# Grouped-query softmax attention: a first Q load in three pieces, fewer warm-up matmuls, and a last normalisation and store on other engines

## The chip, the cores and the metric

The kernel runs on one core of one Trainium2 chip. The metric is the device time of one execution in microseconds (us), median of several runs.

## The reference, cut to what matters

```python
B, Hq, Hkv, Sq, Sk, D = 16, 16, 8, 384, 384, 256       # all bf16
def reference(q, k, v):
    k = jnp.repeat(k, 2, axis=1); v = jnp.repeat(v, 2, axis=1)
    scores = jnp.einsum("bhqd,bhkd->bhqk", q, k) * D ** -0.5
    p = softmax(scores, axis=-1)
    return jnp.einsum("bhqk,bhkd->bhqd", p, v)
```

There are 128 **head pairs** (a batch and a kv head, with its two query heads). Each has six **units** of 128 query rows, 768 units in all. The pipeline works in **steps** of two units, 384 steps, three to a head pair. In the prediction "p=1" is the second head pair; "the last pair" and "the first tail pair" there mean two units, a step.

## The kernel before

Each engine has its own program, and semaphores tie them together. For one step: PE multiplies Q by K (scores S), DVE takes the negative row maximum (`negm`), ACT takes the exponential, PE transposes the result, DVE copies it out of PSUM, PE multiplies it by V (O, with a column of ones in V giving the row sum), ACT evicts O to SBUF, DVE takes the reciprocal of the row sum, POOL multiplies, and POOL stores to DRAM once per head pair. SP issues all loads. POOL also multiplies K by the scale.

```python
QB = KB = VB = 3; ...; NWARM = 24; KS_LEAD = 4         # cut
# SP: per head pair p
sp.dma_start_transpose(KTsb[:, p % KB], k[b, kvh]).then_inc(sem_k[p % KB], 16)
sp.dma_start_transpose(QTsb[:, p % QB], q[...]).then_inc(sem_q[p % QB], 16)
sp.dma_start(Vsb[:, p % VB, :, 0:D], v[...]).then_inc(sem_v[p % VB], 16)
# PE
for _w in range(NWARM):
    pe.matmul(psum[:, 7, 0:512], lhsT=ones[:, 0:128], rhs=ones[:, 0:512], ...)
for i in range(0, ND + 3):                             # do_S(i), do_O(i-2), do_PT(i-1); cut
# DVE, step i:  copy of P (i-2), reciprocal (i-3), max (i)
# ACT, step i:  two exponentials (i-1), then the eviction of O (i-2):
act.activation(out=Of32[:, ..., 0:D + 1], in_=psum[:, b0:b0 + 2, OOFF:OOFF + D + 1], func=ACT.Identity)
# POOL
pool.tensor_scalar(out=Osb[...], in0=Of32[...], scalar1=recip[:, g:g + 1], ...)     # norm of unit g
if g % UPP == UPP - 1:                                 # last unit of the head pair
    pool.wait_ge(sem_norm, g + 1)
    pool.dma_start(out[b, ...], Osb[:, p % OB]...).then_inc(sem_ost[p % OB], 16)
...
for s in range(OB):                                    # POOL's last act: all stores landed
    pool.wait_ge(sem_ost[s], 16 * n)
```

## Time and profile before

| | before |
|---|---|
| time, median of the first 4 runs | 651.22 us |
| span of the profiled run | 649.4 us |
| PE busy | 639.9 us (99%) |
| start of the first scores | 8.54 us |
| start of the second head pair's scores (step 3) | 13.32 us |
| start of the last step's scores | 638.42 us |
| from there to the end | 10.98 us |

From the page of the kernel before, the busy time of each engine, with its share of the span and its number of instructions:

```profile
PE 639.9 (99%) x6168; PEld 513.1 (79%) x6168; DVE 599.1 (92%) x1536; ACT 592.8 (91%) x1153; POOL 557.9 (86%) x1031
```

PE bounds the middle. A step takes 1.645 us there (median distance between the scores of neighbouring steps), and from the second head pair's scores to the last step's scores it is 638.42 - 13.32 = 625.10 us. Nothing in the change touches that stretch. What can move is the 13.3 us in front and the 11.0 us behind.

The start, from the timeline of the kernel before. The columns are start (us), length (us), engine (SPq is SP's sequencer, where the length is the time that issuing took), line, operation, tiles, shape and count; neighbours of one kind are merged:

```profile
0.80 1.32 SPq L98 DMA_TRANSPOSE KTsb<-in_k_dram  x1
1.38 7.33 PE L163 MATMUL psum<-ones 128*128 128x512 bf16 x24 [1.38 <-POOL ones L111]
2.18 1.46 SPq L99 DMA_TRANSPOSE QTsb<-in_q_dram  x1
...
5.59 1.92 SPq L99 DMA_TRANSPOSE QTsb<-in_q_dram  x1
...
8.54 1.46 PE L175 MATMUL psum<-KTsb,QTsb 128*128 128x384 bf16 x8
...
13.32 0.81 PE L175 MATMUL psum<-KTsb,QTsb 128*128 128x384 bf16 x4
```

The first Q was issued at 2.18 us and landed 4.04 us later, at 6.22. The scores began only at 8.54, right behind the last warm-up matmul. So the warm-ups held the start back, not the data. The second Q, issued at 5.59, landed at 9.91, over three microseconds before its use at 13.32.

The end, from the timeline of the kernel before:

```profile
638.42 0.81 PE L175 MATMUL psum<-KTsb,QTsb 128*128 128x384 bf16 x4
...
640.42 1.04 ACT L266 ACTIVATE Psb<-psum,negm 128x384 bf16<-128x384 f32 x2
...
642.00 0.83 PE L204 MATMUL psum<-Vsb,PTsb 128*128 128x257 bf16 x6
...
643.77 0.93 POOL L133 TENSOR_SCALAR Osb<-Of,recip 128x256 bf16<-128x256 f32 x2 [0.29 <-DVE recip L243]
644.99 0.76 POOL L140 DMA_DIRECT2D out_dram<-Osb  x1 [0.30 <-POOL Osb L133]
```

And from its view of DMA issues, the last store alone (KB, then us from issue to landing):

```profile
out_dram<-Osb POOLq DMA_DIRECT2D x1, 384.0 KB, 2.9
```

The store landed at 647.88 us. A **drain** (DRAIN) is a sequencer instruction that each engine has once at the kernel's end, recorded at line 49. The view of that line shows POOL's, with its length in ns and its start in us:

```profile
L49 POOLq DRAIN  x1: 1056/1056/1056, 648.1 to 648.1; - x1
```

### The profile page before, as it was taken

The page shows a single profiled execution, that of the slowest core. Times are in us where ns is not written, and L with a number is a line of the kernel's source. Part 1 is how long each engine was busy: PE and PEld are TensorE (multiplying, and loading weights), DVE is VectorE, ACT ScalarE, POOL GpSimd, SP SyncE. Part 2 cuts the span into 40 slices and gives each one's busy share as a digit, 9 for nine tenths or more (in the row PEclk, how much of TensorE's full clock was granted, in tenths as well). Part 3 has the DMA queues.
Part 4 walks back from the last instruction along what each step waited for, and adds up shares of the span by engine and source line. Part 5 has one row for each costly group of instructions (what it writes and reads, how often), then busy time and mean ns, then how long its engine had stood idle before and what let it go on. Part 6 is the DMA issues. An engine that isn't in the chain of part 4 may idle for free. (4 is left out here: it accounts for less than half of the span.)

```text
span 649.4 us, 18750 instructions
## 1 busy us (share of the span) xinstructions
PE 639.9 (99%) x6168; PEld 513.1 (79%) x6168; DVE 599.1 (92%) x1536; ACT 592.8 (91%) x1153; POOL 557.9 (86%) x1031
## 2 busy tenths in 40 slices
PE   8999999999999999999999999999999999999995
PEld 4888888888888888888888888888888888888884
DVE  3999999999999999999999999999999999999995
ACT  3999999999999999999999999999999999999995
POOL 3878898898888888889888988988888898898886
PEclk9999999999999999999999999999999999999999
DMA  8999999999999999999999999999999999999992
GB/s 164 207 222 268 233 235 261 240 226 266 231 226 262 223 254 224 265 233 223 245 254 234 229 266 238 223 266 230 237 255 232 240 228 267 234 225 259 236 218 97
DMA packets 368735, 152.23 MB, mean 234 GB/s; under 512 B 307200, under 2 KB 358400, under 8 KB 368640
## 3 DMA queue, kind: packets, MB, share of 16 engines
q1 hardware_dynamic: 354304, 100.70, 87.0%
q0 software_dynamic: 14336, 50.34, 21.2%
q8 instruction: 50, 0.82, 0.6%
q14 instruction: 45, 0.37, 0.2%
HBM read 25.17 MB, written 50.33 MB: 116 GB/s over the span
## 5 line engine op out<-in xcount | busy, mean ns | idle before, releaser
L266 ACT ACTIVATE Psb<-psum,negm 128x384 bf16<-128x384 f32 x768 | 401.0, 578 | 8.3 <-DVE negm L251 8.3
L251 DVE TENSOR_REDUCE negm<-psum 128x2 f32<-128x768 f32 x384 | 367.6, 958 | 42.3 <-PE psum L175 9.7
L133 POOL TENSOR_SCALAR Osb<-Of,recip 128x256 bf16<-128x256 f32 x768 | 353.0, 473 | 20.2 <-DVE recip L243 2.6
L204 PE MATMUL psum<-Vsb,PTsb 128*128 128x257 bf16 x2304 | 316.1, 273 | 0.5 <-DVE PTsb L235 0.3
L175 PE MATMUL psum<-KTsb,QTsb 128*128 128x384 bf16 x1536 | 312.2, 326 | 0.0
L204 PEld LDWEIGHTS psum<-Vsb,PTsb 128*128 128x128 bf16 x2304 | 225.2, 98 | 66.9 <-DVE PTsb L235 0.8
L277 ACT ACTIVATE Of<-psum 128x514 f32<-128x514 f32 x384 | 231.0, 602 | 41.6 <-PE psum L204 1.7
L235 DVE COPY PTsb<-psum 128x384 bf16<-128x384 bf16 x768 | 235.2, 348 | 1.1 <-PE psum L190 0.9
L190 PE MATMUL psum<-ident,Psb 128*128 128x128 bf16 x2304 | 191.6, 219 | 1.1 <-ACT Psb L266 1.0
L175 PEld LDWEIGHTS psum<-KTsb,QTsb 128*128 128x128 bf16 x1536 | 140.4, 103 | 45.9
L190 PEld LDWEIGHTS psum<-ident,Psb 128*128 128x128 bf16 x2304 | 160.8, 97 | 11.2 <-ACT Psb L266 1.7
L140 POOL DMA_DIRECT2D out_dram<-Osb x128 | 97.5, 762 | 41.0 <-POOL Osb L133 37.4
L122 POOL TENSOR_SCALAR KTsb<-KTsb 128x768 bf16<-128x768 bf16 x128 | 106.3, 830 | 26.0 <-DMA KTsb<-in_k_dram 16.2
L243 DVE RECIPROCAL recip<-Of 128x2 f32<-128x2 f32 x384 | 59.8, 156 | 1.2 <-ACT Of L277 1.2
L163 PE MATMUL psum<-ones 128*128 128x512 bf16 x24 | 7.3, 478 | 1.4 <-POOL ones L111 1.4
L163 PEld LDWEIGHTS psum<-ones 128*128 128x128 bf16 x24 | 2.8, 119 | 5.4 <-issue 2.7
L266 ACT ACT_TABLE_LOAD x1 | 1.3, 1283 | 0.8 <-PEq L294 0.8
L111 POOL MEMSET ones<- 128x512 bf16 x1 | 0.5, 524 | 0.3 <-POOLq L294 0.3
L294 POOL MEMSET const-float32-0.0<- 128x1 f32 x1 | 0.1, 93 | 0.3 <-issue 0.3
L114 POOL TENSOR_SCALAR_AFFINE_SELECT ident<-ones 128x128 bf16<-128x128 bf16 x1 | 0.3, 291 | 0.1
L112 POOL MEMSET Vsb<- 128x72 bf16 x1 | 0.2, 161 | 0.0
L294 POOL MEMSET const-uint8-127<- 128x1 uint8 x1 | 0.1, 96 | 0.0
(2 smaller groups left out, 0.2 us busy)
## 6 DMA issues: line engine op xcount, KB each, us to landing
out_dram<-Osb POOLq DMA_DIRECT2D x128, 384.0 KB, 4.2
Vsb<-in_v_dram SPq DMA_DIRECT2D x128, 192.0 KB, 3.8
KTsb<-in_k_dram SPq DMA_TRANSPOSE x128, 4.2
QTsb<-in_q_dram SPq DMA_TRANSPOSE x128, 4.8
```

The costliest lines, as they stand in the source:

```text
L122: pool.tensor_scalar(out=kt_ap, in0=kt_ap, scalar1=scale, scalar2=1.0, op0=ALU.mult, op1=ALU.mult,).then_inc(sem_ks, 1)
L133: pool.tensor_scalar(out=Osb[:, p % OB, j, t, :], in0=Of32[:, g % OFB, 0:D], scalar1=recip[:, g:g + 1], scalar2=1.0, op0=ALU.mult, op1=ALU ...
L140: pool.dma_start(out[b, kvh * REP:(kvh + 1) * REP].rearrange("h (p t) d -> p h (t d)", p=128), Osb[:, p % OB].rearrange("p h t d -> p h (t ...
L163: pe.matmul(psum[:, 7, 0:512], lhsT=ones[:, 0:128], rhs=ones[:, 0:512], start=True, stop=True)
L175: ins = pe.matmul(psum[:, sbank, 0:Sk], lhsT=QTsb[:, p % QB, dt, j * Sq + t: (j + 1) * Sq: QT], rhs=KTsb[:, p % KB, dt, :], start=(dt == 0 ...
L190: ins = pe.transpose(psum_bf[:, bank, kt * 128:(kt + 1) * 128], Psb[:, g % PB, kt * 128:(kt + 1) * 128], ident[:],)
L204: ins = pe.matmul(psum[:, bank, OOFF:OOFF + D + 1], lhsT=PTsb[:, g % PTB, kt, :], rhs=Vsb[:, p % VB, kt, 0:D + 1], start=(kt == 0), stop=( ...
L235: dve.tensor_copy(out=PTsb[:, g % PTB].rearrange("p a b -> p (a b)"), in_=psum_bf[:, PTO_BANK0 + g % NPTO, 0:KT * 128],).then_inc(sem_ptev, 1)
L243: dve.reciprocal(out=recip[:, g:g + 2], in_=Of32[:, g % OFB:g % OFB + 2, D:D + 1],).then_inc(sem_recip, 1)
L251: dve.tensor_reduce(out=negm[:, g:g + 2], in_=psum[:, b0:b0 + 2, 0:Sk], axis=AX.X, op=ALU.max, negate=True,).then_inc(sem_max, 1)
L266: act.activation(out=Psb[:, g % PB, :], in_=psum[:, S_BANK0 + g % NSB, 0:Sk], func=ACT.Exp, bias=negm[:, g:g + 1], scale=1.0,).then_inc(se ...
L277: act.activation(out=Of32[:, g % OFB:g % OFB + 2, 0:D + 1], in_=psum[:, b0:b0 + 2, OOFF:OOFF + D + 1], func=ACT.Identity,).then_inc(sem_oc, 1)
```

## The change

Its intent is to shorten both ends. In front: 14 warm-ups instead of 24; the first head pair's Q in three loads (128, 256 and 384 rows), so that its first unit could start early; and no wait for POOL's scaling of the first K, the scale being applied on ACT instead, to `negm` and in the exponential. Behind: the last three steps are normalised on ACT directly from PSUM, with DVE's reciprocal also from PSUM, and the last head pair is stored by SP, one store per head. The diff, cut to its core:

```diff
-    NWARM = 24
+    NWARM = 14
+        Q0_PIECES = [(0, 0, 128), (0, 128, Sq)] + [(j, 0, Sq) for j in range(1, REP)]
+        TAIL0 = NU - UPP
 # SP
+                if p == 0:
+                    for i, (j, r0, r1) in enumerate(Q0_PIECES):
+                        sp.dma_start_transpose(
+                            QTsb[:, 0, :, j * Sq + r0:j * Sq + r1], q[b, kvh * REP + j, r0:r1, :]
+                        ).then_inc(sem_q0[i], 16)
 ...
+            for j in range(REP):                       # the last head pair, one store per head
+                sp.wait_ge(sem_tn, QT * (j + 1))
+                sp.dma_start(out[b, kvh * REP + j]..., Osb[:, pl % OB, j]...).then_inc(sem_ostt[j], 16)
+            for j in range(REP):
+                sp.wait_ge(sem_ostt[j], 16)
 # POOL
+                if g >= TAIL0:
+                    return                             # no norm and no store of the last head pair
-                if e % DPP == 0 and e // DPP < NP:
+                if e % DPP == 0 and 1 <= e // DPP < NP:    # the first K is not scaled
                     do_ks(e // DPP)
-                n = len([p for p in range(NP) if p % OB == s])
+                n = len([p for p in range(NP - 1) if p % OB == s])
 # DVE, step i, after the max
+                if 0 <= e < ND and 2 * e >= TAIL0:     # e = i - 2
+                    for g in (2 * e, 2 * e + 1):
+                        dve.reciprocal(out=recip[:, g:g + 1], in_=psum[..., OOFF + D:OOFF + D + 1])
 # ACT, the first three steps
+                                act.activation(out=negm0[:, g:g + 2], in_=negm[:, g:g + 2], func=ACT.Identity, scale=scale)
+                                act.activation(out=Psb[...], in_=psum[...], func=ACT.Exp, bias=negm0[:, g:g + 1], scale=scale)
 # ACT, the last three steps, after the exponentials
+                        act.activation(out=Osb[:, p % OB, j, t, :], in_=psum[..., OOFF:OOFF + D],
+                                       func=ACT.Identity, scale=recip[:, g:g + 1])
```

Left out: the first head pair's row order and the store that fits it, and the waits of PE that follow from all this.

More of the change, by code (lines that the diff above doesn't have):

```diff
@@ L88, in bass_standalone__gqa_softmax__near_ridge_kernel, with q0_piece, q_count @@
         sem_norm = sem("sem_norm")
+        Q0_PIECES = [(0, 0, 128), (0, 128, Sq)] + [(j, 0, Sq) for j in range(1, REP)]
+        sem_q0 = [sem(f"sem_q0_{i}") for i in range(len(Q0_PIECES))]
+        sem_at = sem("sem_at")
+        negm0 = sb("negm0", [128, UPP], F32)
+        def q0_piece(j, t):
+            for i, (jj, r0, r1) in enumerate(Q0_PIECES):
+                if jj == j and r0 <= t * 128 < r1:
+                    return i
+            raise AssertionError
+        sem_rct = sem("sem_rct")
+        sem_tn = sem("sem_tn")
+        sem_ostt = [sem(f"sem_ostt{j}") for j in range(REP)]
+        TAIL0 = NU - UPP
+        def q_count(p):
+            n = p // QB + 1
+            if p % QB == 0:
+                n -= 1
+            return 16 * n
         block = es.enter_context(nc.Block())
@@ L98, in _ @@
                 sp.dma_start_transpose(KTsb[:, p % KB], k[b, kvh]).then_inc(sem_k[p % KB], 16)
-                sp.dma_start_transpose(
-                    QTsb[:, p % QB], q[b, kvh * REP:(kvh + 1) * REP].rearrange("h s d -> (h s) d")
-                ).then_inc(sem_q[p % QB], 16)
+                if p == 0:
[3 more added lines that the diff above has]
+                        ).then_inc(sem_q0[i], 16)
+                else:
+                    sp.dma_start_transpose(
+                        QTsb[:, p % QB], q[b, kvh * REP:(kvh + 1) * REP].rearrange("h s d -> (h s) d")
+                    ).then_inc(sem_q[p % QB], 16)
                 if p >= VB:
@@ L107, in _ @@
                 ).then_inc(sem_v[p % VB], 16)
+            pl = NP - 1
+            b, kvh = pair_bh(pl)
+            for j in range(REP):
+                sp.wait_ge(sem_tn, QT * (j + 1))
+                if pl == 0:
+                    sp.dma_start(
+                        out[b, kvh * REP + j].rearrange("(t p) d -> p t d", p=128),
+                        Osb[:, pl % OB, j],
+                    ).then_inc(sem_ostt[j], 16)
+                else:
+                    sp.dma_start(
+                        out[b, kvh * REP + j].rearrange("(p t) d -> p (t d)", p=128),
+                        Osb[:, pl % OB, j].rearrange("p t d -> p (t d)"),
+                    ).then_inc(sem_ostt[j], 16)
+            for j in range(REP):
+                sp.wait_ge(sem_ostt[j], 16)
         @block.gpsimd
@@ L139, in do_norm @@
                     pool.wait_ge(sem_norm, g + 1)
-                    pool.dma_start(
-                        out[b, kvh * REP:(kvh + 1) * REP].rearrange("h (p t) d -> p h (t d)", p=128),
-                        Osb[:, p % OB].rearrange("p h t d -> p h (t d)"),
-                    ).then_inc(sem_ost[p % OB], 16)
+                    if p == 0:
+                        pool.dma_start(
+                            out[b, kvh * REP:(kvh + 1) * REP].rearrange("h (t p) d -> p h t d", p=128),
+                            Osb[:, p % OB],
+                        ).then_inc(sem_ost[p % OB], 16)
+                    else:
+                        pool.dma_start(
+                            out[b, kvh * REP:(kvh + 1) * REP].rearrange("h (p t) d -> p h (t d)", p=128),
+                            Osb[:, p % OB].rearrange("p h t d -> p h (t d)"),
+                        ).then_inc(sem_ost[p % OB], 16)
             n_ks = 0
@@ L168, in do_S @@
                 if g % UPP == 0:
-                    pe.wait_ge(sem_ks, p + 1)
-                    pe.wait_ge(sem_q[p % QB], 16 * (p // QB + 1))
+                    if p > 0:
+                        pe.wait_ge(sem_ks, p)
+                        pe.wait_ge(sem_q[p % QB], q_count(p))
+                    else:
+                        pe.wait_ge(sem_k[0], 16)
+                if p == 0:
+                    pe.wait_ge(sem_q0[q0_piece(j, t)], 16)
                 if g >= NSB:
@@ L176, in do_S @@
                         psum[:, sbank, 0:Sk],
-                        lhsT=QTsb[:, p % QB, dt, j * Sq + t: (j + 1) * Sq: QT],
+                        lhsT=(QTsb[:, p % QB, dt, j * Sq + t * 128: j * Sq + (t + 1) * 128] if p == 0
+                              else QTsb[:, p % QB, dt, j * Sq + t: (j + 1) * Sq: QT]),
                         rhs=KTsb[:, p % KB, dt, :],
@@ L186, in do_PT @@
                 if g % 2 == 0 and e >= NPTO // 2:
-                    pe.wait_ge(sem_oc, e - NPTO // 2 + 1)
+                    e2 = e - NPTO // 2
+                    if 2 * e2 >= TAIL0:
+                        pe.wait_ge(sem_tn, 2 * e2 + 2 - TAIL0)
+                    else:
+                        pe.wait_ge(sem_oc, e2 + 1)
                 bank = PTO_BANK0 + g % NPTO
@@ L239, in _ @@
                 e = i - 3
-                if 0 <= e < ND:
+                if 0 <= e < ND and 2 * e < TAIL0:
                     g = 2 * e
@@ L254, in _ @@
                     ).then_inc(sem_max, 1)
+                e = i - 2
+                if 0 <= e < ND and 2 * e >= TAIL0:
+                    for g in (2 * e, 2 * e + 1):
+                        dve.wait_ge(sem_O, g + 1)
+                        dve.reciprocal(
+                            out=recip[:, g:g + 1], in_=psum[:, PTO_BANK0 + g % NPTO, OOFF + D:OOFF + D + 1],
+                        ).then_inc(sem_rct, 1)
         @block.scalar
@@ L265, in _ @@
                             act.wait_ge(sem_PT, g - PB + 1)
-                        act.activation(
-                            out=Psb[:, g % PB, :], in_=psum[:, S_BANK0 + g % NSB, 0:Sk],
-                            func=ACT.Exp, bias=negm[:, g:g + 1], scale=1.0,
-                        ).then_inc(sem_exp, 1)
-                e = i - 2
-                if 0 <= e < ND:
+                        if g < UPP:
+                            if g % 2 == 0:
+                                act.activation(
+                                    out=negm0[:, g:g + 2], in_=negm[:, g:g + 2], func=ACT.Identity, scale=scale,
+                                ).then_inc(sem_at, 1)
+                                act.wait_ge(sem_at, e + 1)
+                            act.activation(
+                                out=Psb[:, g % PB, :], in_=psum[:, S_BANK0 + g % NSB, 0:Sk],
+                                func=ACT.Exp, bias=negm0[:, g:g + 1], scale=scale,
+                            ).then_inc(sem_exp, 1)
+                        else:
+                            act.activation(
+                                out=Psb[:, g % PB, :], in_=psum[:, S_BANK0 + g % NSB, 0:Sk],
+                                func=ACT.Exp, bias=negm[:, g:g + 1], scale=1.0,
+                            ).then_inc(sem_exp, 1)
+                e = i - 2
+                if 0 <= e < ND and 2 * e >= TAIL0:
+                    for g in (2 * e, 2 * e + 1):
+                        p, j, t = unit(g)
+                        act.wait_ge(sem_rct, g - TAIL0 + 1)
+                        if g == TAIL0 and p >= OB:
+                            act.wait_ge(sem_ost[p % OB], 16 * (p // OB))
+                        ins = act.activation(
+                            out=Osb[:, p % OB, j, t, :], in_=psum[:, PTO_BANK0 + g % NPTO, OOFF:OOFF + D],
+                            func=ACT.Identity, scale=recip[:, g:g + 1],
+                        )
+                        ins.then_inc(sem_tn, 1)
+                elif 0 <= e < ND:
                     g = 2 * e
```

## The prediction

> **What bounds it now.** The middle is a steady pipeline: in the timeline, one step (two units) starts every 1.643 us, from about 11.7 us to 639 us. PE is busy 99% of the span (busy table); ACT has 1.04 us (exponentials) + 0.60 us (eviction of O) per step, nearly full too. 384 steps of 1.643 us are 631 us, and the change touches none of them beyond the first three and last three. Only the ends, about 18 us of the 649.4 us span, can shrink. The 651.1 - 649.4 = 1.7 us outside the span stay.
>
> **Start, before (timeline).** 24 warm-up matmuls run from 1.38 to 8.7 us; the first scores matmul starts at 8.54. K landed at about 3.7 us (issue 0.80 + 2.9) and all of Q at about 6.2 (2.18 + 4.0). So the warm-up, not the data, holds the start back, by about 2.3 us.
>
> **Start, after.** Warm-ups start every 0.427 us until about 5.5 us and every 0.213 us after it. That agrees with the Trainium skill, "TensorE: Matmul & The Clock Gate", What's actually happening (half rate until about 3.4 us of sustained work). So 14 end at about 6.4 us: scores start 2.1 us earlier, with a warm clock. The Q split barely matters: a K transpose takes 1.21-1.32 us to issue, Q's of twice the rows 1.46-1.56, so most of an issue is fixed; three pieces take an estimated 3.3 us instead of 1.46. Piece 2 would land at about 7.4, just in time. SP's later issues slip by about 1.9 us: the next Q, landed at 9.9 before, would land at 11.4-11.9, needed at about 11.6. Estimated loss 0-0.3 us. The added scaling of negm on ACT (estimated 0.2 us each, three times) lies on the first chain max -> exp -> transpose: 0.2-0.5 us given back. Net: about -1.6 us. Taking K's scaling off POOL is worth nothing: it ended 3.8 us before use.
>
> **End, before.** Last O matmul ends 642.83; eviction, reciprocal, two POOL norms, then the output DMA issue at 644.99, landing +2.9 (issues view), and 1.5 us more to the span's end.
>
> **End, after.** The last pair's norm goes from PSUM on ACT, estimated at 0.85 us a pair instead of 0.60. The reciprocal of the first tail pair is queued on DVE behind the last max (ended 640.23), and the last exponentials wait behind that pair's norms: about +0.7 us on the last transposes and O. Then reciprocal, one norm, and an SP DMA of half the size, issued at an estimated 644.3, landing in about 2.2 us (V's loads under load took 2.6-2.9; the skill's "DMA: Bandwidth & Descriptors", Specifications, gives the sync path a shorter first-byte latency than the gpsimd path). Net: about -1.3 us.
>
> **Sum.** -1.6 - 1.3 = -2.9 us: 648.3 us, eight in ten between 646.8 and 649.7. Chances: faster by over 2% 0.005, within 2% 0.99, slower 0.005.
>
> **What would show it.** First scores matmul at 6.3-6.6 us; a wait of the p=1 scores for Q under 0.4 us; step still 1.643 us; in the end, the last exponential about 0.8 us later relative to the last scores; last DMA issue on SP about 5.9 us after the last scores matmul starts (before: 6.6).
>
> **What would make it wrong.** A longer cold clock; Q pieces or the next Q landing later, which stalls PE; pair 0's store in 512-byte rows disturbing POOL; the tail chain on ACT costing more than the shorter DMA saves.

## The result, and the profile after

The changed kernel takes 647.08 us (median of 9 runs, 646.78 to 647.25) against 651.23 us (13 runs, 650.63 to 652.27). The ratio is 0.9934, 95% interval 0.9925 to 0.9943, about 4.2 us. Ratios here are the mean time of one kernel's fast runs over that of the other's of the same rounds, so not quite the ratio of the medians quoted. The profiled span went from 649.4 to 645.3 us. The prediction's 648.3 us was too high, but its range (646.8 to 649.7) holds the result, close to the lower edge.

The busy line of the changed kernel:

```profile
PE 638.1 (99%) x6158; PEld 511.8 (79%) x6158; DVE 599.7 (93%) x1539; ACT 594.2 (92%) x1159; POOL 553.6 (86%) x1023
```

The middle is what it was: from the second head pair's scores to the last step's scores it is 637.20 - 12.11 = 625.09 us. The whole difference lies at the ends. The start, from the timeline of the changed kernel:

```profile
1.38 4.95 PE L213 MATMUL psum<-ones 128*128 128x512 bf16 x14 [1.38 <-POOL ones L153]
2.19 3.85 SPq L121 DMA_TRANSPOSE QTsb<-in_q_dram  x3
6.17 1.14 PE L230 MATMUL psum<-KTsb,QTsb 128*128 128x384 bf16 x6
7.82 0.50 PE L230 MATMUL psum<-KTsb,QTsb 128*128 128x384 bf16 x2 [0.51 <-DMA QTsb<-in_q_dram]
7.98 1.49 SPq L125 DMA_TRANSPOSE QTsb<-in_q_dram  x1
10.54 0.83 POOL L164 TENSOR_SCALAR KTsb<-KTsb 128x768 bf16<-128x768 bf16 x1 [8.76 <-DMA KTsb<-in_k_dram]
12.11 0.81 PE L230 MATMUL psum<-KTsb,QTsb 128*128 128x384 bf16 x4 [0.77 <-POOL KTsb L164]
```

The first scores start 2.37 us earlier, yet the second head pair's scores start only 1.21 us earlier (12.11 against 13.32): 1.16 us is given back. Three pieces took 3.85 us to issue where one load took 1.46, so the second Q left SP at 7.98 instead of 5.59. PE then stood idle for 0.77 us before 12.11. The view puts this down to POOL's scaling of the second K. But that scaling ended at 11.37, and a wait for several semaphores has to be checked against all of them. The second Q, issued at 7.98, took this long to land, by the view of DMA issues of the changed kernel:

```profile
QTsb<-in_q_dram SPq DMA_TRANSPOSE x1, 4.0
```

It landed at 12.02 us by the trace's record of its semaphore, 0.09 us before the scores began. So it was that Q that PE waited for. The second K came late with it (landed at 10.46, against 8.37 before). Without the wait for Q, its scaling on POOL, done at 11.37, would, by these numbers, have been the next thing to hold these scores.

PE also waited 0.51 us for the third piece of the first Q, which landed at 7.77. That cost nothing: the first transposes (8.88) came 2.71 us after the first scores, as they do in warm18 below, where no such wait occurs.

The end, from the timeline of the changed kernel, and its last store in the view of DMA issues:

```profile
637.20 0.81 PE L230 MATMUL psum<-KTsb,QTsb 128*128 128x384 bf16 x4
...
639.12 0.84 ACT L355 ACTIVATE Osb<-psum,recip 128x256 bf16<-128x256 f32 x2 [0.51 <-DVE recip L319]
...
639.85 1.05 ACT L344 ACTIVATE Psb<-psum,negm 128x384 bf16<-128x384 f32 x2
...
641.28 0.97 PE L264 MATMUL psum<-Vsb,PTsb 128*128 128x257 bf16 x6
...
642.02 0.94 ACT L355 ACTIVATE Osb<-psum,recip 128x256 bf16<-128x256 f32 x2 [0.39 <-DVE recip L319]
```

```profile
out_dram<-Osb SPq DMA_DIRECT2D x1, 192.0 KB, 1.9
```

From the last step's scores to the end it is now 645.35 - 637.20 = 8.15 us instead of 10.98, a gain of 2.83 us. It comes although the last exponentials start later after those scores (2.65 us instead of 2.00), because they queue on ACT behind two norms. The last store is issued at 642.99 and lands at 644.87; the span ends 0.48 us after that, not 1.52.

The view of line 49 shows the drains of the changed kernel:

```profile
L49 POOLq DRAIN  x1: 1137/1137/1137, 643.1 to 643.1; - x1
L49 SPq DRAIN  x1: 7/7/7, 645.1 to 645.1; - x1
```

The single instruction records give the same times to two decimals. This table is made from them and is not one of the profile's views. Times are us from the span's start.

| | before | after |
|---|---|---|
| last store issued | 644.99, POOL | 642.99, SP |
| last store landed | 647.88 | 644.87 |
| POOL's closing drain | 648.11 to 649.17 | 643.10 to 644.24 |
| end of the last record | 649.4 | 645.3 |

Before, POOL waited for the landing and only then drained, for 1.06 us, in series: that is 1.06 of the 1.52 us. After, it is SP that waits, and POOL's drain (1.14 us) is over before the landing.

Two theories had to be tested. **In front** ("SP queue"): the split itself takes back the microsecond, by delaying the second head pair's loads in SP's queue. The rivals are that the loads could not come faster in any case ("supply"), and that the new scaling of `negm` on ACT costs it ("ACT"). **Behind** ("drain"): a large part of the gain is POOL's closing drain leaving the last chain. The rival ("landing") is that only the shorter norm chain and the faster store count.

### The profile page after: what moved, and what is told of

It is laid out like the page before. It is cut to its first block, busy times and chain, and to the rows that moved or that the text cites. A ratio compares the mean times of both kernels' runs of the same rounds, so it can differ in the third digit from the quotient of the medians.

```text
span 645.3 us, 18736 instructions
## 1 busy us (share of the span) xinstructions
PE 638.1 (99%) x6158; PEld 511.8 (79%) x6158; DVE 599.7 (93%) x1539; ACT 594.2 (92%) x1159; POOL 553.6 (86%) x1023
## 4 chain that ended last, share of the span: by engine, by line
PE 97%; SPq 1%; DMA 1%; ACT 0%; issue 0%; DVE 0%; POOL 0%; DVEq 0%
PE psum L264 39%; PE psum L230 38%; PE psum L250 20%; SPq L121 1%; DMA KTsb<-in_k_dram 1%; ACT Osb L355 0%; SPq L118 0%; ACT Psb L344 0%; POOL KTsb L164 0%; DVE negm L311 0%; SPq L130 0%; DVE recip L319 0%; DVEq L294 0%
## 5 line engine op out<-in xcount | busy, mean ns | idle before, releaser
L213 PE MATMUL psum<-ones 128*128 128x512 bf16 x14 | 5.0, 530 | 1.4 <-POOL ones L153 1.4
L355 ACT ACTIVATE Osb<-psum,recip 128x256 bf16<-128x256 f32 x6 | 2.6, 479 | 0.9 <-DVE recip L319 0.9
```

## The experiments

Twelve kernels ran; all were correct. First the readings of all traces in one table. "Slow gaps" counts the distances between starts of neighbouring warm-ups above 0.3 us (most are 0.427 us before the clock rises and 0.216 after; the prediction writes 0.213). The clock records of the traces show the rise at the same place: full clock begins at 5.42 us in the kernel before and at 6.70 in warm14. S1 is the start of the first scores, Q2 the landing of the second head pair's Q, S2 the start of its scores, and "end part" the time from the last step's scores to the end. All are in us.

| kernel | warm-ups | slow gaps | S1 | Q2 | S2 | end part | median time |
|---|---|---|---|---|---|---|---|
| before | 24 | 10 | 8.54 | 9.91 | 13.32 | 10.98 | 651.23 |
| changed | 14 | 9 | 6.17 | 12.02 | 12.11 | 8.15 | 647.08 |
| warm14 | 14 | 13 | 7.02 | 9.60 | 11.79 | 10.99 | 649.58 |
| tail_only | 24 | 11 | 8.90 | 9.66 | 13.67 | 8.15 | 648.50 |
| wait_on_sp | 24 | 8 | 8.14 | 9.86 | 12.92 | 10.26 | 650.31 |
| store_on_sp | 24 | 7 | 8.00 | 9.58 | 12.78 | 9.17 | 650.00 |
| pool_waits | 14 | 8 | 6.04 | 12.20 | 12.29 | 9.31 | 648.41 |
| one_q | 14 | 11 | 6.69 | 9.70 | 11.70 | 8.14 | 646.36 |
| one_q_pool_scale | 14 | 10 | 6.55 | 9.58 | 11.32 | 8.14 | 646.13 |
| warm18 | 18 | 12 | 7.81 | 12.21 | 12.82 | 8.16 | 647.91 |
| tail4 | 14 | 13 | 7.17 | 12.30 | 12.39 | 7.56 | 646.57 |
| best14 | 14 | 8 | 6.25 | 9.46 | 11.02 | 7.54 | 645.58 |
| best12 | 12 | 11 | 6.39 | 9.50 | 11.17 | 7.53 | 645.61 |
| v_on_act | 10 | 9 | 5.62 | 10.71 | 10.80 | 7.57 | 645.13 |

Two things to read at once. S1 varies by some 0.9 to 1.1 us between kernels with the same number of warm-ups (8.00 to 8.90 with 24, 6.04 to 7.17 with 14), because the clock rises after 7 to 13 slow gaps (in v_on_act all 9 were slow and the clock rose only at 6.05 us, after S1). And wherever Q2 is at 10.7 us or later, S2 is Q2 + 0.09 us, with one exception (warm18). There S1 no longer counts.

The kernel before had these medians in the rounds of the three groups of runs: 651.85 us (warm14, tail_only, wait_on_sp, one_q), 651.73 us (pool_waits, warm18, one_q_pool_scale, tail4) and 651.20 us (store_on_sp and the last three). Ratios below are against those. Each group ran on another chip, so medians of different groups are compared only with care.

### warm14: fewer warm-ups alone

```diff
-    NWARM = 24
+    NWARM = 14
```

> The kernel before with 14 warm-up matmuls instead of 24 and nothing else. Theory 'SP queue' (the changed kernel loses part of its earlier start because the split of the first Q adds two issues on SP, which makes the second pair's Q land at 12.0 us): unsplit, nothing slips, so the first scores start at 6.2-6.3 us, the second pair's scores at 11.0-11.1 us (13.32 before) and the whole 2.3 us is kept: 648.9 us. Rival 'supply' (the loads can't come faster in any case): second pair's scores near 12.1 us, 650.0 us.

649.58 us, ratio 0.9965 (0.9951 to 0.998): about 2.3 us (1.3 to 3.2 by the interval), in line with the 2.2 us that ten warm-ups take at 0.216. From the timeline of this run:

```profile
7.02 1.46 PE L175 MATMUL psum<-KTsb,QTsb 128*128 128x384 bf16 x8
...
11.79 0.81 PE L175 MATMUL psum<-KTsb,QTsb 128*128 128x384 bf16 x4
```

The first scores came at 7.02, not at the expected 6.2-6.3, because in this run all 13 gaps were slow. Still, from S1 to S2 it is 4.77 us, as before (4.78), and Q2 landed at 9.60. So with the loads unsplit the earlier start is kept in full. The time and S2 as they stand are nearer to the rival's numbers (650.0 us, 12.1) than to the first expectation (648.9 us, 11.0). What tells against supply is that Q2 had landed 2.19 us before S2; and in best14, below, S2 came at 11.02 with unsplit loads. In the traces this one line gave more at the start than all of the start changes together (S2 at 11.79 against 12.11), although its clock rose later.

### tail_only: the end alone

```diff
 # the changed kernel with NWARM = 24, one Q load, K of the first head pair scaled on POOL,
 # and no scaling on ACT: everything of the start as before
```

> The kernel before with the end of the change alone (norm of the last three pairs of units on ACT, two stores from SP); the start is as before. If the two ends add up, the gain is what the traces show from the last scores to the end, 10.98 - 8.1 = 2.9 us: 648.3 us. If start and end interact, it differs by more than 0.3 us.

648.50 us, ratio 0.9954 (0.9933 to 0.9975): 3.0 us (1.6 to 4.4). The end part is 8.15 us, the same as in the changed kernel. The end keeps its gain on its own. The two halves, 2.3 and 3.0 us, would sum to 5.3 us, and the change gave about 4.2. These intervals are too wide to show a missing microsecond by the clock. The traces show it: from S1 to S2 it is 5.94 us in the changed kernel and 4.77 here, and the end part is the same, so the loss lies in the other parts of the start.

### one_q: the changed kernel with one Q load

```diff
-        Q0_PIECES = [(0, 0, 128), (0, 128, Sq)] + [(j, 0, Sq) for j in range(1, REP)]
+        Q0_PIECES = [(0, 0, REP * Sq)]                 # and one transposing load of q[b, both heads]
```

> The changed kernel with the first Q loaded in one transposing load instead of three. Theory 'SP queue': Q lands at 6.2 us, the second pair's Q at about 9.9 us, its scores start at 11.2-11.5 us instead of 12.11, and the time falls by 0.6-0.9 us to about 646.3 us. Rival 'ACT' (the three scalings of negm on ACT cost the lost microsecond): no change beyond 0.1 us, 647.1 us.

646.36 us, ratio 0.992 (0.9907 to 0.9932), 0.7 us below the changed kernel's median. The two sets of times overlap (646.21 to 647.52 here), so the trace has to decide. From the timeline of this run:

```profile
6.69 1.46 PE L230 MATMUL psum<-KTsb,QTsb 128*128 128x384 bf16 x8
...
11.70 0.81 PE L230 MATMUL psum<-KTsb,QTsb 128*128 128x384 bf16 x4
```

Q2 landed at 9.70 instead of 12.02, and S2 came 0.41 us earlier although S1 was 0.52 us later. S2 was expected at 11.2-11.5; the slower clock phase of this run (11 slow gaps) accounts for the rest. From S1 to S2 it is 5.01 us instead of 5.94. The scaling on ACT is still in this kernel, so it cannot have cost these 0.93 us. The split did.

### one_q_pool_scale: also without the scaling on ACT

```diff
 # on top of one_q
-                if e % DPP == 0 and 1 <= e // DPP < NP:
+                if e % DPP == 0 and e // DPP < NP:     # POOL scales the first K again
-                        if g < UPP:                    # ACT: negm0, scale=scale
+                        if False:
```

> The changed kernel with the first Q in one load and the first K scaled on POOL again, so without the scaling of negm on ACT. With the loads out of the way the start is set by the chain scores, max, exponential, transpose, on which the scaling adds 0.23-0.25 us: about 0.2 us below the run with one Q load alone, 646.1 us. If that scaling costs nothing, 646.4 us.

646.13 us, ratio 0.9913 (0.9892 to 0.9934). The times alone cannot tell this from one_q, but the trace can: from S1 to S2 it is 11.32 - 6.55 = 4.77 us here, as in the kernels without that scaling, and 5.01 us in one_q. The scaling on ACT costs 0.24 us at the start. Putting K's scaling back on POOL cost nothing visible.

### warm18: four more warm-ups in the changed kernel

```diff
-    NWARM = 14
+    NWARM = 18
```

> The changed kernel with 18 warm-up matmuls instead of 14. Theory 'SP queue': the second pair's Q, landing at about 12.0 us, sets the pace, so the first scores may start about 0.85 us later at little cost: at most 0.2 us, 647.1-647.3 us. Rival (the start of the first scores sets the pace): four warm-ups of 0.213 us, +0.85 us, 647.9 us.

647.91 us (647.02 to 650.23, six runs), ratio 0.9945 (0.9924 to 0.9967): a miss, for this is the rival's number. From the timeline of this run:

```profile
7.81 1.46 PE L230 MATMUL psum<-KTsb,QTsb 128*128 128x384 bf16 x8
...
12.82 0.81 PE L230 MATMUL psum<-KTsb,QTsb 128*128 128x384 bf16 x4
```

Q2 landed at 12.21 us, but S2 came at 12.82, which is S1 + 5.01, the distance that one_q also has. So the later of the two governs: Q2's landing, or S1 + 5.01 us. The changed kernel has slack only up to an S1 of about 7.1, and I had taken the distance to be about 4.7. Two of the six runs, 647.02 and 647.08, were as fast as the changed kernel. This profile also holds two stalls of 0.54 and 0.79 us in the middle of the run, near 358 and 364 us, which no other of these traces has in this size. Their cause was not settled, and the span of this run is not used.

### wait_on_sp: SP waits for the last stores of the kernel before

```diff
 # moved from the end of POOL's program to the end of SP's
-                    pool.wait_ge(sem_ost[s], 16 * n)
+                    sp.wait_ge(sem_ost[s], 16 * n)
```

> The kernel before, where SP instead of POOL waits for the landing of the last stores; every load, store and norm is the same. Theory 'drain' (POOL's closing drain of 1.06 us ran after the landing, in series, and no longer does): POOL drains while the store is in flight, and the span ends about 0.4-0.5 us after the landing instead of 1.5: 1.0-1.1 us less, 650.1 us. Rival 'landing' (the end gained because SP's store lands faster and the norm chain is shorter): no change, 651.2 us.

650.31 us, ratio 0.9976 (0.9964 to 0.9988). The end part fell from 10.98 to 10.26 us; the rest of the gain in the profiled run is its earlier S1 (8 slow gaps instead of 10). The store is the same one from POOL, issued at 644.62 and landed at 647.50 (2.88 us). From the landing to the end it was 0.78 us instead of 1.52. So a gain comes with nothing of the norms or the store changed, which the landing rival denies. But it was 0.7 us, not 1.0-1.1: POOL's drain ran from 644.59 to 648.05 and ended 0.55 us after POOL's own store had landed. It looks as if this drain also waits for POOL's own store; one run does not settle that, and it stays open.

### pool_waits: POOL waits again, in the changed kernel

```diff
 # at the end of POOL's program, added
+            for j in range(REP):
+                pool.wait_ge(sem_ostt[j], 16)
```

> The changed kernel, where POOL too waits for the landing of SP's last stores before it ends. Theory 'drain': POOL's closing drain (1.1 us, over before the landing in the changed kernel) comes back into series behind the landing, and the span grows by about 1.1 us, to about 648.2 us. Rival 'landing' (only the faster store and the shorter norm chain matter): no change, 647.1 us.

648.41 us (648.37 to 648.59), ratio 0.9948 (0.9929 to 0.9967), 1.3 us above the changed kernel's median. The end part is 9.31 us instead of 8.15, so 1.16 us more; the remaining 0.18 us is S2, at 12.29. In the records the last store landed at 645.05 and POOL's drain ran from 645.32 to 646.46 (1.14 us); in the view of line 49:

```profile
L49 POOLq DRAIN  x1: 1137/1137/1137, 645.3 to 645.3; - x1
```

The last store took 1.88 us, as in the changed kernel, and nothing but the wait was changed. So the drain theory stands, and the landing rival, that nothing else counts, falls.

### store_on_sp: the kernel before with its last store from SP

```diff
 # POOL: no store of the last head pair; SP, at its end:
+            sp.wait_ge(sem_norm, NU)
+            sp.dma_start(out[...], Osb[:, p % OB]...).then_inc(sem_ostt, 16)
+            sp.wait_ge(sem_ostt, 16)
```

> The kernel before with its last store (384 KB, one piece, after the same POOL norms) issued by SP instead of POOL, and waited for by SP. It splits the gain at the end (2.9 us in the traces): if the drain's place and the sync path's faster store make most of it, 1.5-1.9 us are gained, 649.5 us; if the norm from PSUM on ACT and the store in halves make most of it, under 1 us, 650.4 us.

650.00 us, ratio 0.9973 (0.9959 to 0.9987). The median lies between the two expectations and does not choose; the trace does. The last store of this run, from its view of DMA issues:

```profile
out_dram<-Osb SPq DMA_DIRECT2D x1, 384.0 KB, 2.5
```

The end part is 9.17 us. With the landings from the records this splits the whole gain at the end, all in us:

| | before | store_on_sp | changed |
|---|---|---|---|
| last scores to issue of the last store | 6.57 | 6.31 | 5.79 |
| issue to landing | 2.89 | 2.45 | 1.88 |
| landing to end | 1.52 | 0.41 | 0.48 |
| sum | 10.98 | 9.17 | 8.15 |

Handing one store to SP is worth 1.81 us of the 2.83, of which 1.11 us is the time behind the landing. The norms on ACT and the store in halves give the other 1.02 us.

### tail4: only two steps normalised on ACT

```diff
-        TAIL0 = NU - UPP
+        TAIL0 = NU - 4
 # SP, before the first of the two stores
+                if j == 0:
+                    sp.wait_ge(sem_norm, TAIL0)
-                sp.wait_ge(sem_tn, QT * (j + 1))
+                sp.wait_ge(sem_tn, QT * (j + 1) - (UPP - 4))
```

> The changed kernel with only the last two pairs of units, not three, normalised on ACT from PSUM (the third last goes the old way over POOL). In the changed kernel the last exponentials started at 639.85 us, behind two norms that waited for DVE and took 0.84 us; with the one eviction of 0.60 us, which need not wait for the reciprocal, they start about 0.5 us earlier, and so does all that follows: 646.6 us. If those norms are not on the chain that ends last, 647.1 us.

646.57 us, ratio 0.9921 (0.99 to 0.9943). From the timeline of this run:

```profile
639.01 0.60 ACT L368 ACTIVATE Of<-psum 128x514 f32<-128x514 f32 x1
639.51 1.05 ACT L346 ACTIVATE Psb<-psum,negm 128x384 bf16<-128x384 f32 x2
```

The last exponentials start 639.51 - 637.50 = 2.01 us after the last scores, as before the change, instead of 2.65. The end part is 7.56 us, 0.59 us shorter. The changed kernel normalised one step too many on ACT.

### best14, best12: the better parts together

```diff
 # one_q_pool_scale with TAIL0 = NU - 4 as in tail4; best12 also:
-    NWARM = 14
+    NWARM = 12
```

> The changed kernel with the first Q in one load, the first K scaled on POOL and only the last two pairs of units normalised on ACT: all three found better alone. If they add up, 0.5 us below the run with one Q load and POOL scale: 645.6 us; if the tail's gain is lost to something new, 646.1 us.

> The same with 12 warm-ups. They end at 5.5-6.5 us, by the phase in which the clock rises, and Q lands at 6.1-6.2 us: the start becomes bound by Q, 0.2-0.4 us earlier and with less spread: 645.3 us. If the clock then falls back or rises late, slower than 14.

best14: 645.58 us, ratio 0.9911 (0.9898 to 0.9925); the parts add up (S1 to S2 4.77 us, end part 7.54 us). best12: 645.61 us, the same ratio, so no gain and no less spread (645.34 to 646.28). In its profile all 11 gaps were slow, and the warm-ups still ended after Q had landed (S1 at 6.39, Q at 6.02). In best14's profile the clock rose early (at 4.81 us), and S1 (6.25) seems to have waited for Q already: Q landed at 6.11, and S1 came 0.38 us after the start of the last warm-up instead of 0.22. The times do not tell 12 warm-ups from 14.

### v_on_act: two Q loads, the first V issued by ACT

```diff
 # on top of best12
-    NWARM = 12
+    NWARM = 10
-        Q0_PIECES = [(0, 0, REP * Sq)]
+        Q0_PIECES = [(j, 0, Sq) for j in range(REP)]   # one load per head
 # ACT, first thing; SP loads V only for p > 0
+            act.wait_ge(sem_q0[0], 16)
+            act.dma_start(Vsb[:, 0, :, 0:D], v[0, 0]...).then_inc(sem_v[0], 16)
```

> The same with 10 warm-ups, the first Q in two loads by head, and the first V issued from ACT, so that SP's queue is no longer than with one Q load. Theory 'SP queue': a split is harmless when another issue leaves the queue; first scores at 5.5-5.7 us, the second pair's Q lands by 10.4 us, its scores at 10.4-10.7: 644.8 us. If the split itself (more, smaller loads) is the harm, or the clock stays low, 645.5 us or more.

645.13 us (645.02 to 645.22), ratio 0.9903 (0.9889 to 0.9916): the fastest of all, though 0.3 us above what was expected. From the timeline of this run:

```profile
5.62 1.36 PE L231 MATMUL psum<-KTsb,QTsb 128*128 128x384 bf16 x6
6.14 1.35 SPq L125 DMA_TRANSPOSE QTsb<-in_q_dram  x1
...
10.80 0.81 PE L231 MATMUL psum<-KTsb,QTsb 128*128 128x384 bf16 x4
```

With one issue taken out of SP's queue and only two pieces, the second Q leaves at 6.14 instead of 7.98, lands at 10.71, and S2 follows at 10.80. The start is bound by that landing again, and the spread is small again (four runs). The three edits of this kernel were not run apart, so how much each gives is not shown.

## Why the prediction was right or wrong

The time was right within its range: 648.3 us predicted, 647.08 measured, range 646.8 to 649.7. The gain was underestimated, 2.9 us against about 4.2 by the clock and 4.1 by the spans. Two terms were mis-sized, in opposite directions, and that kept the result inside the range, which is luck: with the start as forecast (-1.6 instead of -1.21) and the end as measured, the time would have been about 646.7 us, just outside.

- **What bounds it, and that only the ends can move: right.** The middle is 625.10 us before and 625.09 after.
- **The warm-ups hold the start, ten fewer are worth 2.1 us: right.** S1 fell by 2.37 us, of which about 0.2 us is one slow gap less; warm14 gives about 2.3 us.
- **"Estimated loss 0-0.3 us" from SP's queue: mis-sized.** The three pieces took 3.85 us to issue, not 3.3, and the second Q landed at 12.02, not at 11.4-11.9. It was also needed earlier than the 11.6 assumed: S1 + 5.01 = 11.18, with the distance that one_q and warm18 show. That makes 0.93 us lost. "A wait of the p=1 scores for Q under 0.4 us" was wrong; it was 0.77. The split did not merely "barely matter": it cost 0.93 us and gave nothing that the traces show, since the first scores come 0.22 us after the start of the last warm-up with it and without it (one_q).
- **"0.2-0.5 us given back" by the scaling on ACT: right**, 0.24 us. With the 0.93 us it makes up the 1.16 us given back at the start; but in the changed kernel taking it out alone would gain nothing, as the wait for Q would stay. "Taking K's scaling off POOL is worth nothing": right (one_q_pool_scale).
- **Start, net -1.6 us: measured -1.21** (13.32 to 12.11).
- **End, the longer chain on ACT, "+0.7 us": right.** The last O matmul ended 4.42 us after the last scores before, 5.05 us after (+0.63). The SP issue was foreseen at 5.9 us after the last scores and came at 5.79. The store's flight was foreseen at 2.2 us and took 1.88. (The 2.6-2.9 us for V's loads on which the 2.2 leans are fast ones; the median of all 128 in the kernel before is 3.8.)
- **End, "1.5 us more to the span's end": the main step that failed.** The prediction read these 1.5 us before the change and carried them over as fixed. 1.06 us of them were POOL's closing drain, in series behind POOL's own wait; once SP held that wait they were 0.48 us. pool_waits puts the drain back (+1.16 us). The end gave 2.83 us, not 1.3: 1.04 us of the difference is this step, 0.3 us the shorter flight, and 0.1 us the earlier issue.

Together: -1.21 - 2.83 = -4.04 us, the difference of the spans. One thing was not foreseen at all: the changed kernel's times spread over 0.5 us, the kernel before's over 1.6 us in the same comparison. That fits S2 following the second Q's landing and not the warm-ups, whose length varies with the clock. This is argued from the table of traces and not shown; no run was made for it.

## What to carry to other kernels

When a load is split to start earlier, cost the added issues against what queues behind them: here each added transposing load cost 1.2 to 1.3 us of SP's time, for 128 rows as for 384, and the second set of loads became the new limit. At the end of a kernel, look at what each engine still has to do after its last wait, and let an engine that closes quickly hold the wait for the last store. And when a short head or tail is optimised piece by piece, measure each piece alone: two parts of this change measured 2.3 and 3.0 us by themselves, the whole gave 4.2, and the traces put the loss in a third part, the split.

## What the Trainium skill lacked or had wrong

- "VectorE: DVE Perf Modes", The DRAIN you can't avoid, tells two kinds of drain apart: the flush after a vector instruction, and the runtime's own before and after a program, about 12 ns each on all five engines. The closing drains here, which the profile records at a line of the kernel (line 49), fit neither, and the page lacks them: POOL's took 1.06 us (before) and 1.14 us (changed, pool_waits), in series with the end where POOL waited last; PE's and ACT's took 0.5 to 0.6 us, DVE's 0.2, SP's 0.01 (changed, pool_waits). POOL's was longer where it began before POOL's last work was done: 1.74 us in store_on_sp, 3.46 in wait_on_sp.
- No page gives the time that SP needs to issue a transposing load on this chip by its size; "DMA: Bandwidth & Descriptors" has one figure for small tiles on "previous generations", without a size. Here it was 1.22 us for 128 rows of 256 bf16, 1.26 us for 256 and 1.28 us for 384 (changed), so nearly all of it was fixed. The first load of 768 rows took 1.46 us, later ones more (median 1.71 in the kernel before, with other loads in flight).
- "DMA: Bandwidth & Descriptors", Anatomy of one DMA, fits the gpsimd path as 2.0 us plus bytes over 436 GB/s, an estimated 2.90 us for 384 KB. The last store took 2.89 us (before), so this agrees where little else is in flight; the median of all 128 stores was 4.2 us. It has no such fit for the sync path: 384 KB took 2.45 us and 192 KB 1.88 us when issued from SP. That SP's store is the faster one agrees with what the prediction cites.
- "TensorE: Matmul & The Clock Gate", What's actually happening, says that the number of slow matmuls at the start varies from run to run, with 6, 11 or 14 in one kernel. This agrees: 7 to 13 slow gaps in 14 traces. The 3.4 us of sustained work that the prediction takes from the same section are no fixed length here: from the first warm-up to the rise in the clock records it took 4.04 us in the kernel before, and in all traces 2.95 (store_on_sp) to 5.62 us (tail4). What it lacks is the size of the effect on a short prologue: with 14 warm-ups the first scores moved between 6.04 and 7.17 us.
